# A three-stage fp32 kernel on one core: the low part of the spatial weights by accumulating transfers, stage-two weights stored negated, and a table of 253 offsets

## The chip, the core and the metric

The kernel runs on one core of a Trainium2 chip. Its engines each run their own queue in order: TensorE (PE) multiplies matrices, VectorE (DVE), ScalarE (ACT) and GpSimd (POOL) work on tiles, SyncE (SP) issues most of the DMA transfers and GpSimd a few. The metric is the device time of one execution in microseconds. Before the change three runs gave 916.47, 917.31 and 918.84 us; the median is 917.31.

## The reference

Three blocks follow each other, in float32, for 8 batches of 576 positions:

```
q_s = softmax(q, axis=-1); k_s = softmax(k, axis=seq)      # 8 heads of 64
x   = q_s @ (k_s^T @ v)                                    # block 1: [8, 576, 512]
h   = gelu(x @ w_in); u, v = halves of h                   # block 2: w_in 512 x 1024
v_n = layernorm(v) * g_ln
v_s = einsum('ts,bsd->btd', w_sg, v_n) + b_sg              # w_sg 576 x 576: the spatial weights
x   = x + (u * v_s) @ w_out
h   = relu(x @ w_in2)                                      # block 3
out = (h * sigmoid(conv3(h, conv_w))) @ w_out2
```

The weights of blocks 2 and 3 are read by the kernel as they come, and the first thing done with each is to take it apart into two numbers.

## The kernel before

**Products in three parts.** A float32 product on TensorE is made of three products of a shorter type (fp32r): each operand is a high part, which is the value rounded to that type, and a low part, which is what the rounding left. `mm3` multiplies high by high, high by low and low by high into one accumulator. So every weight and every activation is needed as a pair: `wAh` and `wAl` in the rows are the pair of `w_in`, `wouth` and `woutl` of `w_out`, `sgh` and `sgl` of the spatial weights, `vnh` and `vnl` of the normalized `v`, `gh` and `gl` of the gated product, `xh` and `xl` of a batch's activations.

**Who makes the pairs.** For an activation ScalarE copies the value to the short type (high) and VectorE subtracts (low). For the weights of block 2 (`split`, a job of 1024 columns) ScalarE and VectorE rebuild the value from a 64-bit layout in six steps, ScalarE rounds it, and TensorE then makes the low part of 512 columns in a group of three products into one accumulator: the value times `one` (the unit matrix, a full float32 product), and two products with `neg` (the unit matrix with its sign turned) that subtract the parts that are there; ScalarE copies the result out. One job gives two such groups. The jobs of `w_in` and `w_out` share their working tiles: the tiles `xh` and `xl` of a batch that has not begun, halves of `vnh` and `vnl`, and `wsl`. The rows of the order show `xl` in this part.

**The spatial weights** (`sg_split`, `sg_tail`) come as 4 chunks of 128 x 576 and a tail of 64 x 576, loaded into one `q` tile (the tail into `x2s`). For each chunk ScalarE rounds the high part; for each half of 288 columns TensorE adds raw times `one` and high times `neg` (`part`), and ScalarE copies the result to `sgl`. The tail goes the same way, and its low part is copied to two tiles, `rhs`. That makes ten groups of two products. The bias of the spatial product, `b_sg`, is split by ScalarE and VectorE and sent into two rows of `rhs` by way of DRAM.

**The loops.** Block 1 loads `k`, `v` and `q` per batch, takes maxima and sums on VectorE, subtracts and multiplies on GpSimd, takes exponentials on ScalarE, and `xt` writes `xh` and `xl`. GpSimd's subtraction of the maxima (`kt<-kt,scr`) comes in runs of up to seven instructions that stand in a row. Block 2 runs per batch: `hv` (the products that give `v`, with `norm`), then for each of 8 tiles `hu` (12 products that give `u`), `mx` (14 products with the spatial weights; VectorE multiplies with `u`, ScalarE makes `gh`, VectorE makes `gl`), and `wo` (12 products with `w_out` that read `gh` and `gl`). The sum goes to DRAM as `x2d`, once by a plain transfer and once by a transfer of `xl` that GpSimd issues and that adds to what stands there. While block 2 works on one batch, block 1 of the next is laid between its products. Block 3 reads `x2d` back and repeats per tile: `h2`, the convolution (`cv`), the gate, and `o2`.

**What sets the order.** The kernel's functions do not issue instructions; a recorder (`Plan`) keeps each as a node with what it depends on, and all are issued at the end from one place, so nearly all rows of the profile have one line, L486 (after the change the same place is L488). `price` gives each node a cost, `deadlines` counts back from TensorE's order when each must start, and a table, `MOVED`, adds an offset in microseconds to this due time for chosen nodes (`node:offset`). `order` then plays the program through: whenever an engine is free it takes the ready node that is due first, and TensorE's units of products (a `hu`, an `mx`, a group) are put off while their inputs are late. What an engine has been given by this play it runs in that order on the chip.

## Time and profile before

| what | value |
|---|---|
| median of three runs | 917.31 us (916.47 to 918.84) |
| the profiled execution | 917.11 us, its span 915.3 us |
| TensorE busy | 894.4 us, 98% of the span |
| VectorE, ScalarE, GpSimd busy | 720.7, 536.5, 275.6 us |
| granted TensorE clock in 40 slices of the span | 9 tenths or more in each |

The span is what the profiler saw from the first to the last instruction; the time is counted by the device and lies 1.8 us above it. The busy share is an average over stages: in the first slice of 22.9 us TensorE is busy for five tenths, then for nine tenths or more up to the last slice. Idle time of an engine that nothing waits for costs nothing, which holds for most of what ScalarE and GpSimd have. In the chain that ended last TensorE holds 88% of the span and VectorE 6%, so what remains is to be looked for where TensorE stands still.

### The profile page before, as it was taken

How to read it: one execution, taken by the hardware profiler on the slowest of the kernel's cores; microseconds unless marked ns; L12 is line 12 of the kernel's file. 1: busy time of each engine (PE TensorE's matmuls, PEld its weight loads, DVE VectorE, ACT ScalarE, POOL GpSimd, SP SyncE). 2: the span in 40 equal slices, each digit the busy share in tenths (PEclk: the TensorE clock that was granted, in tenths of full speed). 3: DMA queues.
4: the chain of work that ended last, by engine and by line, in shares of the span. 5: the costliest groups of instructions: out<-in, count | busy, mean ns of one | idle time of the engine just before them, and what ended most of it. 6: DMA issues, size and time to landing. Idle time of an engine off the chain costs nothing.

```text
span 915.3 us, 15835 instructions
## 1 busy us (share of the span) xinstructions
PE 894.4 (98%) x6158; PEld 802.7 (88%) x6158; DVE 720.7 (79%) x1269; ACT 536.5 (59%) x1081; POOL 275.6 (30%) x251
## 2 busy tenths in 40 slices
PE   5999999999999999999999999999999999999997
PEld 4688989988889888898999998988999889888996
DVE  6898998887886898888655389898878878875783
ACT  7886476566456555464524155446677666766673
POOL 5044364644535546374422001102020202020000
PEclk9999999999999999999999999999999999999999
DMA  9932458463743736422857441102021202020001
GB/s 315 273 128 48 136 111 243 114 166 99 185 107 100 201 93 212 107 74 93 226 200 218 129 120 52 47 8 102 6 93 34 76 1 94 6 98 13 13 35 57
DMA packets 51235, 101.50 MB, mean 111 GB/s; under 512 B 8788, under 2 KB 22228, under 8 KB 49368
## 3 DMA queue, kind: packets, MB, share of 16 engines
q1 hardware_dynamic: 46408, 89.87, 30.2%
q0 software_dynamic: 4752, 10.62, 6.9%
q8 instruction: 48, 0.79, 0.4%
q14 instruction: 27, 0.22, 0.1%
HBM read 62.59 MB, written 37.88 MB: 110 GB/s over the span
## 4 chain that ended last, share of the span: by engine, by line
PE 88%; DVE 6%; DMA 3%; ACT 1%; SPq 1%; issue 1%; POOL 0%; POOLq 0%; ACTq 0%; DVEq 0%
PE mm L486 58%; PE acc L486 30%; DVE gl L486 2%; DMA x2d<-xl 1%; DMA wsl<-in_w_in 1%; DMA x2d<-x2s 1%; SPq L486 1%; DMA sgh<-in_q 1%; DVE xl L486 1%; DVE u L486 0%; DVE r L486 0%; DVE scr L486 0%; DVE qm L486 0%; DVE wsl L486 0%; DVE q L486 0%
## 5 line engine op out<-in xcount | busy, mean ns | idle before, releaser
L486 DVE SCALAR_TENSOR_TENSOR cv<-h,cw,cv 128x576 f32<-128x576 f32 x128 | 109.9, 860 | 16.9 <-ACT cv L486 14.5
L486 PE MATMUL acc<-wAh,yl 128*128 128x512 f32 x256 | 101.8, 398 | 0.2 <-DVE yl L486 0.2
L486 PE MATMUL acc<-wAl,yh 128*128 128x512 f32 x256 | 101.0, 395 | 0.0
L486 PE MATMUL acc<-wAh,yh 128*128 128x512 f32 x256 | 100.7, 393 | 0.0
L486 POOL TENSOR_TENSOR q<-q,qm 128x576 f32<-128x576 f32 x56 | 68.8, 1254 | 56.9 <-DVE qm L486 25.5
L486 PE MATMUL mm<-xh,w2h 128*128 128x288 f32 x280 | 83.0, 297 | 0.0
L486 PE MATMUL mm<-xh,w2l 128*128 128x288 f32 x280 | 82.4, 294 | 0.0
L486 PE MATMUL mm<-xl,w2h 128*128 128x288 f32 x280 | 82.4, 294 | 0.0
L486 PE MATMUL acc<-gl,wouth 128*128 128x288 f32 x256 | 76.1, 297 | 3.3 <-DVE gl L486 3.3
L486 PE MATMUL mm<-xh,wAh 128*128 128x288 f32 x256 | 76.5, 299 | 0.0
L486 PE MATMUL acc<-gh,wouth 128*128 128x288 f32 x256 | 76.4, 299 | 0.0
L486 PE MATMUL mm<-sgh,vnh 128*128 128x288 f32 x256 | 76.0, 297 | 0.2 <-DVE u L486 0.2
L486 PE MATMUL acc<-gh,woutl 128*128 128x288 f32 x256 | 75.8, 296 | 0.0
L486 PE MATMUL mm<-xh,wAl 128*128 128x288 f32 x256 | 75.6, 295 | 0.0
L486 PE MATMUL mm<-xl,wAh 128*128 128x288 f32 x256 | 75.6, 295 | 0.0
L486 PE MATMUL mm<-sgh,vnl 128*128 128x288 f32 x256 | 75.5, 295 | 0.0
L486 PE MATMUL mm<-sgl,vnh 128*128 128x288 f32 x256 | 75.4, 295 | 0.0
L486 ACT ACTIVATE gh<-u 128x288 fp32r<-128x288 f32 x64 | 28.1, 442 | 74.0 <-DVE u L486 62.1
L486 ACT ACTIVATE cv<-cv 128x576 f32<-128x576 f32 x64 | 43.7, 683 | 40.7 <-DVE cv L486 40.3
L486 DVE TENSOR_TENSOR gl<-u,gh 128x288 fp32r<-128x288 f32 x64 | 53.1, 834 | 10.7 <-ACT gh L486 10.6
L486 DVE TENSOR_TENSOR u<-mm,u 128x288 f32<-128x288 f32 x64 | 28.9, 453 | 39.6 <-PE mm L486 39.3
L486 POOL TENSOR_TENSOR kt<-kt,scr 128x512 f32<-128x512 f32 (+1 forms) x42 | 47.4, 1150 | 38.0 <-DVE scr L486 25.8
(302 smaller groups left out, 2757.1 us busy)
## 6 DMA issues: line engine op xcount, KB each, us to landing
x2d<-x2s SPq DMA_DIRECT2D x16, 576.0 KB, 4.0
x2d<-xl POOLq DMA_DIRECT2D x8, 1152.0 KB, 9.0
kt<-in_k SPq DMA_DIRECT2D x7, 1152.0 KB, 10.5
q<-in_q SPq DMA_DIRECT2D x28, 288.0 KB, 3.8
xf<-x2d SPq DMA_DIRECT2D x7, 1152.0 KB, 5.2
vt<-in_v SPq DMA_DIRECT2D x7, 1024.0 KB, 8.1
out<-ot SPq DMA_DIRECT2D x28, 256.0 KB, 2.0
wsl<-in_w_in SPq DMA_DIRECT2D x9, 512.0 KB, 5.4
```

The source lines that it names most:

```text
L486: getattr(self.real[n.eng], n.name)(*[val(a) for a in n.args], **{k: val(v) for k, v in n.kw.items()})
```

## The change

**Spatial weights.** The high part is now stored with its sign turned (ScalarE's copy with a factor of -1). `gather` has GpSimd issue a transfer from one tile in SBUF into another that adds to what stands there: high part, negative, onto the raw weights, so that the low part is left in their place. Three such transfers are issued, for chunks 0 and 1, chunks 2 and 3 (576 KB each) and the tail (288 KB). ScalarE copies the result, with a factor of -1, into `sgl` chunk by chunk and into the two `rhs`. The ten groups of TensorE and their twelve copies are gone.

**Sign.** `split` for the weights of block 2 stores all parts negated, with `neg` where `one` stood in the first product of a group; `b_sg` is negated as well. The two Gelu instructions that read these products (`norm` and `hu`) have a factor of -1; where two negated operands meet, the signs cancel.

**Scheduling.** The costs of two kinds of nodes in `price` are changed (a copy with a running sum, a transfer issued by GpSimd), and `MOVED` holds 253 other offsets; the node numbers count anew, since the nodes of the spatial weights differ. A branch `far` in `split` is added that no job uses (`JOBS` holds only `n`).

```diff
-JOBS = 'nnnnnnnnnnnn'
-SGL = 'nnnn'
+JOBS = 'nnnnnnnnnn'
+SGA = ((0, 1), (2, 3))
...
 MOVED = """
-6:-16.1 7:-20.3 9:-42.4 10:-15.1 11:-4.8 12:-5.9 13:5.3 17:-6.7 20:-32.7 28:5.7 31:32.3 35:3.8 41:-15.1 44:4.9 53:-5.4 87:4.4 142:-22.8 166:4.7
...
+6:-45.6 7:-28.9 8:-89.8 9:-47.9 10:-44.5 11:-35.2 13:-33.9 14:-17.7 15:-42.8 20:-50.1 28:-16.7 31:-61.1 32:-44.2 34:-17.8 35:-17.4 37:-24.3 50:-42.6
...
             if "accum_out" in n.kw:
-                n.cost += 0.1
+                n.cost += 0.19
...
             if "dma" in name:
-                n.cost, n.lat = 1.34, 9.3
+                n.kb, n.rate = views[0].ids.size * 4 / 1024, 186
+                n.cost, n.lat = 1.34, 3.1 + n.kb / n.rate
                 return
...
             if n.eng == "pool" and "dma" in n.name:
-                wire[0] = max(t + 1.2, wire[0]) + 6.2
+                wire[0] = max(t + 1.2, wire[0]) + n.kb / n.rate
...
+    def gather(out, part):
+        pool.dma_start(out, r32(part), accum_op=ALU.add, max_dma_last_dim=2304)
+
...
         if hi is not None:
-            act.activation(hi, a, AF.Copy)
+            act.activation(hi, a, AF.Copy, scale=-1.0 if summed else 1.0)
...
         if summed:
-            dve.scalar_tensor_tensor(lo, l, -(2.0 ** -52), hf, ALU.mult, ALU.mult)
+            dve.scalar_tensor_tensor(lo, l, 2.0 ** -52, hf, ALU.mult, ALU.mult)
...
-                pe.matmul(ps, one, cut(a), start=True, stop=False)
+                pe.matmul(ps, r32(neg), cut(a), start=True, stop=False)
                 pe.matmul(ps, neg, cut(hi), start=False, stop=False)
                 pe.matmul(ps, neg, cut(lo), start=False, stop=True)
...
-        act.activation(vt_, ps, AF.Gelu_apprx_tanh)
+        act.activation(vt_, ps, AF.Gelu_apprx_tanh, scale=-1.0)
...
-        act.activation(u, ps, AF.Gelu_apprx_tanh)
+        act.activation(u, ps, AF.Gelu_apprx_tanh, scale=-1.0)
...
     def sg_split(c):
-        hi, lo, raw = sg["hi"][:, c], sg["lo"][:, c], sgr["t"][:, c]
-        act.activation(hi, raw, AF.Copy)
-        if SGL[c] != 'n':
-            E[SGL[c]].tensor_tensor(lo, raw, r32(hi), ALU.subtract)
-        for hf in range(2 if SGL[c] == 'n' else 0):
-            cs = slice(hf * HALF, hf * HALF + HALF)
-            plan.begin()
-            ps = mm_tile()[:, 0:HALF]
-            part(ps, raw[:, cs], hi[:, cs])
-            act.activation(lo[:, cs], ps, AF.Copy)
+        hi, raw = sg["hi"][:, c], sgr["t"][:, c]
+        act.activation(hi, raw, AF.Copy, scale=-1.0)
+        for g in SGA:
+            if c == g[-1]:
+                cs = slice(g[0], c + 1)
+                gather(sgr["t"][:, cs], sg["hi"][:, cs])
+                for i in g:
+                    act.activation(sg["lo"][:, i], sgr["t"][:, i], AF.Copy, scale=-1.0)
 
     def sg_tail():
-        act.activation(rhs1, sgs[:, 0], AF.Copy)
-        for hf in range(2):
-            cs = slice(hf * HALF, hf * HALF + HALF)
-            plan.begin()
-            ps = mm_tile()[:, 0:HALF]
-            part(ps, sgs[:, 0, cs], rhs1[:, cs])
-            for e in range(2):
-                r = slice(64 * e, 64 * e + 64)
-                act.activation(rhs2[e][r, cs], ps[r], AF.Copy)
+        act.activation(rhs1, sgs[:, 0], AF.Copy, scale=-1.0)
+        gather(sgs[:, 0], rhs1)
+        for e in range(2):
+            r = slice(64 * e, 64 * e + 64)
+            act.activation(rhs2[e][r], sgs[r, 0], AF.Copy, scale=-1.0)
...
-
-    def part(ps, x, hi):
-        pe.matmul(ps, one, x, start=True, stop=False)
-        pe.matmul(ps, neg, hi, start=False, stop=True)
```

**TensorE, before, between the last job of `w_in` and the first of `w_out`.** Of a group of three products on `xl` the last one makes the low part; `hu` and `mx` are units of 12 and 14 rows, of which the first two stand here. The names are those of buffers, each with a number.

```order
L486 MATMUL mm_178<-xl_0_184,one_80 128x512
...
L486 MATMUL mm_131<-xl_0_184,one_80 128x512
...
L486 MATMUL mm_152<-xh_0_306,wAh_297 128x288
L486 MATMUL mm_152<-xl_0_327,wAh_297 128x288
...
L486 MATMUL mm_143<-sgh_388,vnh_528 128x288
L486 MATMUL mm_143<-sgl_488,vnh_528 128x288
...
L486 MATMUL mm_178<-xh_0_306,wAh_297 128x288
L486 MATMUL mm_178<-xl_0_327,wAh_297 128x288
...
L486 MATMUL mm_131<-xl_0_184,one_80 128x512
L486 MATMUL mm_131<-wouth_704,neg_96 128x512
L486 MATMUL mm_131<-woutl_711,neg_96 128x512
```

**TensorE, after, the same place.**

```order
L488 MATMUL mm_153<-xl_0_213,neg_96 128x512
...
L488 MATMUL mm_133<-xh_0_313,wAh_301 128x288
L488 MATMUL mm_133<-xl_0_334,wAh_301 128x288
...
L488 MATMUL mm_180<-xl_0_213,neg_96 128x512
...
L488 MATMUL mm_133<-xh_0_313,wAh_301 128x288
L488 MATMUL mm_133<-xl_0_334,wAh_301 128x288
...
L488 MATMUL mm_153<-xh_0_313,wAh_301 128x288
L488 MATMUL mm_153<-xl_0_334,wAh_301 128x288
...
L488 MATMUL mm_180<-xl_0_213,neg_96 128x512
L488 MATMUL mm_180<-wouth_659,neg_96 128x512
L488 MATMUL mm_180<-woutl_662,neg_96 128x512
```

The two groups of the last `w_in` job stood side by side, with a `hu`, an `mx` and a `hu` (38 products) between them and the `w_out` job. Now a `hu` stands between the two groups, and two `hu` (24 products) between the second group and the `w_out` job.

**ScalarE, before, the same place.** `xl<-xh` is the first step of the `w_out` job, `wouth<-xl` its rounding, `wAl<-mm` copies out a low part of the `w_in` job, `u` and `v` read the Gelu products, `lt` belong to the normalized tail.

```order
L486 ACTIVATE wAl_295<-mm_178 128x4x128
L486 ACTIVATE rd_523<-mv_518 128x1
L486 ACTIVATE xl_0_184<-xh_0_166 128x1024
L486 ACTIVATE lt_0_663<-v_465,rd_523 64x512
L486 ACTIVATE lt_0_109<-v_465,rd_523 64x512
L486 ACTIVATE wAl_295<-mm_131 128x4x128
L486 ACTIVATE u_686<-mm_152 128x288
L486 ACTIVATE qx_638<-qm_578 32x72 x3
L486 ACTIVATE wouth_704<-xl_0_184 128x1024
```

**ScalarE, after, the same place.**

```order
L488 ACTIVATE u_620<-mm_133 128x288
L488 ACTIVATE v_464<-mm_161 128x512
L488 ACTIVATE xl_0_213<-xh_0_127 128x1024
L488 ACTIVATE vnh_518<-v_476,rd_615 128x512
...
L488 ACTIVATE lt_0_373<-xl_0_213 128x512
...
L488 ACTIVATE v_476<-acc_0_278 128x512
...
L488 ACTIVATE u_117<-mm_153 128x288
L488 ACTIVATE wsl_192<-wsl_192 128x512
L488 ACTIVATE lt_0_655<-v_464,rd_615 64x512
L488 ACTIVATE lt_0_106<-v_464,rd_615 64x512
L488 ACTIVATE wouth_659<-xl_0_213 128x1024
```

Between the first step of the `w_out` job and its rounding stood five rows, the third of them a copy of a low part; now ten stand there, among them the eviction of a `v` and of a `u` and the steps of another job (`lt<-xl`, `wsl`). The first step stands behind a `u` and a `v` that read TensorE's products.

On VectorE the rows of the same `w_out` job stand like this after the change: `vnl` (reads what ScalarE writes as `vnh` in the fourth row above), two steps on `xl` in one row each, a third one, `lt` (reads what ScalarE writes in the two rows `lt<-v`), a step that writes `xh`, and the last, which writes `woutl`. Before, `lt` stood behind the first step on `xl`, and the other four steps of the job in a row behind it. GpSimd's runs of `kt` subtractions: between the `mx` whose `gl` VectorE makes beside the second of them and the `wo` that reads this `gl`, TensorE had 67 products and now has 27.

## Rows read from the trace of the kernel before

**Rows 1.** The page of the profile: its span, and the first line of its first part.

```profile
span 915.3 us, 15835 instructions
PE 894.4 (98%) x6158; PEld 802.7 (88%) x6158; DVE 720.7 (79%) x1269; ACT 536.5 (59%) x1081; POOL 275.6 (30%) x251
```

**Rows 2.** Timeline of TensorE, 44 to 71 us: start us, duration us, engine, line, instruction.

```profile
44.86 0.65 PE L486 MATMUL mm<-q,one 128*128 128x288 f32 x2
...
45.48 0.65 PE L486 MATMUL mm<-q,one 128*128 128x288 f32 x2
...
60.98 1.02 PE L486 MATMUL mm<-xl,one 128*128 128x512 f32 x2
...
63.63 0.29 PE L486 MATMUL mm<-xh,wAh 128*128 128x288 f32 x1
...
68.66 1.02 PE L486 MATMUL mm<-xl,one 128*128 128x512 f32 x2
...
70.06 0.50 PE L486 MATMUL mm<-woutl,neg 128*128 128x512 f32 x1 [0.15 <-DVE woutl L486]
```

**Rows 3.** By tile (neg, sgl, x2s): count, ns shortest/median/longest, first and last start.

```profile
L486 PE MATMUL mm<-sgh,neg x8: 508/509/513, 45.1 to 56.6; 128*128 128x288 f32 x8
...
L486 ACT ACTIVATE sgl<-mm x8: 410/410/432, 45.7 to 57.2; 128x288 fp32r<-128x288 f32 x8
...
L486 ACT ACTIVATE rhs<-x2s x1: 685/685/685, 36.5 to 36.5; 128x576 fp32r<-128x576 f32 x1
```

**Rows 4.** DMA issues of the page: count, KB each, median us to landing.

```profile
x2d<-x2s SPq DMA_DIRECT2D x16, 576.0 KB, 4.0
x2d<-xl POOLq DMA_DIRECT2D x8, 1152.0 KB, 9.0
```

**Rows 5.** Timeline of ScalarE, 60 to 69 us, columns as in rows 2.

```profile
60.10 0.67 ACT L486 ACTIVATE lt<-xl 128x512 f32<-128x512 f32 x1
...
61.24 0.60 ACT L486 ACTIVATE v<-mm 128x512 f32<-128x512 f32 x1 [0.19 <-PE mm L486]
...
63.36 1.14 ACT L486 ACTIVATE xl<-xh 128x1024 f32<-128x1024 f32 x1 [0.17 <-PE mm L486]
64.41 1.32 ACT L486 ACTIVATE lt<-v,rd 64x512 fp32r<-64x512 f32 x2
...
66.12 0.38 ACT L486 ACTIVATE u<-mm 128x288 f32<-128x288 f32 x1
...
68.03 1.06 ACT L486 ACTIVATE wouth<-xl 128x1024 fp32r<-128x1024 f32 x1 [0.70 <-DVE xl L486]
```

**Rows 6.** Timeline of VectorE, 52 to 70 us, and one row at 28 us.

```profile
28.47 0.69 DVE L486 TENSOR_TENSOR scr<-kt 128x512 f32<-128x512 f32 x1 [0.69 <-DMA kt<-in_k]
...
52.50 0.72 DVE L486 SCALAR_TENSOR_TENSOR vnl<-v,rd,vnh 128x512 fp32r<-128x512 f32 x1
...
64.54 0.69 DVE L486 TENSOR_SCALAR xl<-xl 128x1024 f32<-128x1024 f32 x1 [0.63 <-ACT xl L486]
...
66.77 1.22 DVE L486 SCALAR_TENSOR_TENSOR xl<-xh,xl 128x1024 uint32<-128x1024 uint32 x1
...
68.76 1.24 DVE L486 SCALAR_TENSOR_TENSOR woutl<-xh 128x1024 fp32r<-128x1024 uint32 x1
```

**Rows 7.** Windows: us, busy us (instructions) by engine, granted clock, DMA share, GB/s.

```profile
0.00:45.00 45.00, 32.72 (x217) 23.04 (x218) 33.71 (x66) 34.19 (x75) 13.68 (x28) 1.00 0.93 293
```

**Rows 8.** Timelines of GpSimd and VectorE, 201 to 208 us.

```profile
201.63 6.67 POOL L486 TENSOR_TENSOR kt<-kt,scr 64x256 f32<-64x256 f32 x6 [4.08 <-DVE scr L486]
...
202.78 4.94 DVE L486 TENSOR_TENSOR gl<-u,gh 128x288 fp32r<-128x288 f32 x1
```

**Rows 9.** Timeline of TensorE: its idle times over 0.5 us behind the first 30 us.

```profile
207.77 0.40 PE L486 MATMUL acc<-gl,wouth 128*128 128x288 f32 x1 [1.67 <-DVE gl L486]
...
272.69 0.40 PE L486 MATMUL acc<-gl,wouth 128*128 128x288 f32 x1 [0.58 <-DVE gl L486]
...
338.85 0.40 PE L486 MATMUL acc<-gl,wouth 128*128 128x288 f32 x1 [0.70 <-DVE gl L486]
```

More of the change, by code (lines that the diff above doesn't have):

```diff
@@ L540, in u64, with split @@
         return ap.bitcast(U32)
-    def split(slot, src, hi, lo, n, modes, stores=(), behind=None):
+    def gather(out, part):
+        pool.dma_start(out, r32(part), accum_op=ALU.add, max_dma_last_dim=2304)
+    def split(slot, src, hi, lo, n, modes, stores=(), behind=None, far=False):
         raw, a = slot
@@ L571, in split @@
             return
+        if far:
+            low = slot[0][:, 0:n]
+            if len(src.shape) == 4:
+                low = low.rearrange("p (g f) -> p g f", g=g)
+            gather(a, hi)
+            dve.scalar_tensor_tensor(low, l, 2.0 ** -52, hf, ALU.mult, ALU.mult)
+            gather(a, low)
+            act.activation(lo, a, AF.Copy, scale=-1.0)
+            return
         if summed:
-            dve.scalar_tensor_tensor(lo, l, -(2.0 ** -52), hf, ALU.mult, ALU.mult)
+            dve.scalar_tensor_tensor(lo, l, 2.0 ** -52, hf, ALU.mult, ALU.mult)
             for o in range(0, n, 512):
@@ L1149, in w_job @@
     def w_job(i):
-        split(slots[ORDER[i]], *jobs[i], None if JOBS[i] == 'n' else (E[JOBS[i]], E[JOBS[i]]))
+        split(slots[ORDER[i]], *jobs[i], None, far=JOBS[i] == 'a')
     n1 = len(PAIR[0])
@@ L1187, in sg_tail @@
         sp.dma_start(bt, b_sg.rearrange("(p f) -> p f", f=9))
-        act.activation(bh, bt, AF.Copy)
-        dve.tensor_tensor(bl, bt, r32(bh), ALU.subtract)
+        act.activation(bh, bt, AF.Copy, scale=-1.0)
+        dve.scalar_tensor_tensor(bl, bt, -1.0, r32(bh), ALU.mult, ALU.subtract)
         for i, t in enumerate((bh, bl)):
```

31 rows, old and new, of the table MOVED are left out of this document.

## The prediction

> **What bounds the kernel now.** I read the page first, for its span and for how busy each engine is; then TensorE's own timeline, for the places where it stands still; then the timelines of ScalarE and VectorE around those places. TensorE is busy for 894.4 of 915.3 us [rows 1], so nothing shortens the kernel that does not take work from TensorE or one of its waits. In the windows view the first 45 us hold 32.72 us of TensorE work [rows 7], so some 12 us of its idle time lie there, while inputs and weights arrive at 293 GB/s and are split. Behind that it waits rarely: in the timeline only three idle times are longer than half a microsecond, 1.67, 0.58 and 0.70 us, all for a `gl` of VectorE [rows 9]. The granted clock is 1.00 in the window shown, the upper of its two levels (2.4 GHz), so no term below is about the clock.
>
> **TensorE's own work.** Before, the low part of the spatial weights takes ten groups: eight for the four main chunks (two halves each) and two for the tail [rows 3]. A group is one fp32 product, which the trace shows as two records, and one with `neg`. Two groups in a row start at 44.86 and 45.48 [rows 2], so a group takes 0.62 us, and ten take 6.2 us. No TensorE instruction comes in their place. In the stretch in which they stand TensorE never waits for long, so they lie on the path that sets the end: 6.2 us is the most that this edit can give by itself. The stored sign costs nothing there: the same products run with `neg` in place of `one`, and ScalarE and VectorE undo it by a factor in instructions that they run anyway.
>
> **ScalarE and the transfers.** ScalarE loses eight copies of 0.41 us and four of half the height, and gains six of 576 columns, 0.69 us each by the one in the trace [rows 3]: 12 times 0.41 against 6 times 0.69 is 0.8 us less, off the path. GpSimd issues three accumulating transfers, of 576, 288 and 576 KB. The trace has no accumulation within SBUF. Its nearest rows are 4.0 us for 576 KB without an addition and 9.0 us for 1152 KB with one [rows 4]; I take 6 us for 576 KB, near the middle. All three are issued in a row on GpSimd, and behind them stands the first power of the normalization; as they leave before that power's input exists, nothing queues. Their results are read on ScalarE by four copies that stand behind a table load and two evictions, and TensorE reads them some 10 us later still. So I count them as hidden. If each took the 9.0 us and ran behind the other, ScalarE would stand up to 3 us, and every weight eviction queued behind it as well: that is the upper end of this term, and zero the lower.
>
> The Trainium skill ("SBUF — State Buffer", section "Who interferes with whom" and the box on the trap above it) speaks against this: descriptors of a transfer issued from GpSimd are written by GpSimd's cores, which a VectorE instruction in a two-port mode locks out, so such a transfer can look several times longer beside a busy VectorE. Here VectorE is busy 33.71 of the first 45 us [rows 7]. The accumulations into `x2d` run beside a VectorE that is busy as well and still land in 9.0 us at the median [rows 4], so this trace does not show the trap; by the rule the sum would be up to 3 us longer, the upper end just given.
>
> **What is late next.** The rows of the program's order in the section on the change matter more than the removed work. M is the last weight job of the first matrix, two groups that read the tile `xl`; the first job of the output weights writes the same tile. Before, that job's first ScalarE step waits for TensorE's last read, starts at 63.36 [rows 5], and its last result arrives for TensorE at 70.06 [rows 2]. Between the two jobs TensorE has work from 63.63 to 68.66, 5.0 us, and so it is 0.3 us late: the first group ends at 70.06 plus 0.23, 1.63 us behind its start, where the two groups of M take 2.65 us together.
>
> After the change only two `hu` units stand between them (24 matmuls of 288 columns; the 38 matmuls from 63.63 to 68.66 give 0.13 each, so 1.6 us for the 12 of a unit), and the job's first ScalarE step stands behind the evictions of the first of these two and of the `v` product. So I count from the end of that first `hu`. ScalarE: `u` 0.38, `v` 0.60, the absolute value 1.14 [rows 5], end at 2.1. VectorE has a `vnl` ahead that waits for one more ScalarE step of some 0.7, and takes 0.72 itself: 3.5. Then two steps of 0.69 and one of 1.22 [rows 6]: 6.1. Its next row, `lt`, needs the first of ScalarE's two `lt`; ten ScalarE instructions stand ahead of `wouth`, by rows 5 0.67, 0.60, 0.38, 0.67 and 1.32 and some small ones, so `lt` comes at about 5.7 and `wouth` ends at 7.4. VectorE goes on with `lt` (as `vnl`, 0.72) to 6.8, one step of 0.7 to 7.5, and `woutl` 1.24 to 8.8. TensorE had the second `hu` until 1.6 and the group of 1.3 until 2.9; it can end the group only at 8.8 plus 0.2. It waits 6.1 us where it waited 0.3: I take +5.7. Bounds: 4.4 if `lt` and `vnl` cost VectorE no waiting, and 8 if GpSimd's subtractions, which now run in that stretch, stretch two VectorE steps by a microsecond each.
>
> **The head.** VectorE takes the key maxima (three rows as that at 28.47, 0.69 us each [rows 6], and a pair of half height) behind the weight splits and no longer between them, so the last of the four first jobs can be ready 2 to 3 us earlier. Against it, a 512 KB weight block is now loaded ahead of the value tiles, 1.8 us at 293 GB/s [rows 7]. Bounds: 2.8 us earlier, 1.8 later. Between its first attention product and the first `hv` TensorE has the same work in both orders, and an earlier weight only helps where it waits for one; so I take little, -0.6, a fifth of the gain's bound.
>
> **The rest** is ordered anew all through by the new offsets, with the same instructions. I take 0 with a bound of 3 us on either side, the sum of the three waits in rows 9.
>
> **Sum.** The profiled execution took 917.1 us, its span of 915.3 and 1.8 around it, and lies 0.2 below the median of the runs (917.31). 917.1 - 6.2 + 5.7 - 0.6 = 916.0.
>
> **Rivals.**
> - The saving stands. If the wait at the output-weight pair is no longer than before, 917.1 - 6.2 - 0.6 gives 910.3; if half of it is hidden, because the head brings the output weights in early enough and ScalarE runs ahead, 913.2. For it: 6.2 us of work really goes. Against it: the order of ScalarE's queue is fixed, and the chain above starts from a TensorE result.
> - GpSimd holds VectorE oftener. GpSimd's run of six subtractions from 201.63 lasts 6.67 us, and a `gl` of VectorE with 288 columns takes 4.94 beside it [rows 8], where a VectorE row with 512 takes 0.72 [rows 6]; that is the wait of 1.67. What decides is how much work TensorE has between `mx` and the `wo` that reads this `gl`. For the second of six such runs the order had 8.9 us of it (67 matmuls at 0.13) and now has 3.6 (27), for the last 12 and now 5.2. From 6.7 us on a run is hidden; at 3.6 it costs 3.1. If the five later runs cost 3.1 and four times 1.67, they cost 9.8 where rows 9 sum to 2.95: 916.0 + 6.8 = 922.8, slower. It is slower by the bound below from 6.9 us on in all.
>   The Trainium skill ("SBUF — State Buffer", "SBUF: two separate sides") says that the loser of the shared port blocks for one whole instruction of the other; the row shows that the `gl` lost to a whole run of them. By the rule a `gl` would lose a sixth of the run, 1.1 us, a time and this rival would vanish; by the row it stands.
> - The transfers land late and ScalarE stands, 3 us as bounded: 919.0. Against it: TensorE needs the result only 10 us later.
>
> **How the numbers follow.** About 0.3% (2.75 us) is what a measurement of this kernel can tell from no change: 914.6 to 920.1. Forecast, most of the saving given back at one new wait: 0.46, with a range of its own of 914 to 918.5. The saving stands wholly or by half: 0.36. GpSimd's runs: 0.12. Late transfers: 0.06. Faster takes the second case and 0.06 of the forecast, its lower edge: 0.42. Slower takes the runs, 0.12. The same is the other 0.40 of the forecast with the late transfers, 0.46. The range reaches to the deeper half of the second case below, 911.0, and to 920.0 above; some 0.1 is left out on each side.
>
> **What would show it.** TensorE's rows lose the ten groups with `q` or `x2s` and `one`, and its busy time falls by about 6. The first group with `wouth` and `neg` has an idle time of some 6 us in front of it or within it, with VectorE or ScalarE named. The four copies into `sgl` show no wait for a transfer over 1 us. The three accumulations land within 4 to 9 us. A `gl` of 4 to 5 us beside each run of subtractions shows whether the third rival grew. The forecast is wrong if the two jobs are further apart in time than their places say, if the first `hv` ends more than 2 us earlier than 44.9, or if the sum of waits for `gl` behind 150 us changes by more than 3.

## The result and the profile after

The changed kernel takes 923.62 us in the median of six runs, the one before 917.35 beside it. The ratio is 1.0064, with a 95% interval of 1.0052 to 1.0076: 0.64% slower. The forecast was 916.0, in a range of 911 to 920, so it was wrong in its sign and in its range.

The first lines of the page of the kernel after; rows 1 has those of before.

```profile
span 921.3 us, 15787 instructions
PE 894.0 (97%) x6128; PEld 799.8 (87%) x6128; DVE 730.3 (79%) x1269; ACT 538.6 (58%) x1077; POOL 280.3 (30%) x254
```

The ten groups are gone, and with them some 6 us of products, yet TensorE is busy for 894.0 us where it was 894.4 [rows 1]. Part of its work therefore ran slower. The windows of the kernel after show where (us, busy us and instructions of TensorE, its weight loads, VectorE, ScalarE, GpSimd, then the granted clock, the DMA share and GB/s):

```profile
62.00:64.00 2.00, 0.00 (x0) 0.00 (x0) 1.93 (x5) 1.95 (x5) 0.00 (x0) 1.00 0.00 0
66.00:68.00 2.00, 1.62 (x2) 0.30 (x2) 1.78 (x4) 2.00 (x3) 0.00 (x0) 0.67 0.00 0
68.00:70.00 2.00, 1.58 (x4) 0.93 (x4) 1.97 (x3) 1.97 (x3) 0.00 (x0) 0.50 0.00 0
...
74.00:76.00 2.00, 2.00 (x18) 2.00 (x17) 1.65 (x3) 1.95 (x5) 0.00 (x0) 1.00 0.00 0
...
406.00:408.00 2.00, 1.25 (x10) 1.01 (x9) 2.00 (x5) 0.00 (x0) 0.05 (x1) 1.00 0.00 0
408.00:410.00 2.00, 2.00 (x10) 2.00 (x10) 1.97 (x6) 1.41 (x2) 0.00 (x0) 0.51 0.62 220
```

At 62 us TensorE does nothing at all for two microseconds, and behind that its clock stands at 0.50, the lower of its two levels (1.2 GHz). It does so again at 408 us. The same two places in TensorE's timeline; the rows at 66.38 and 69.27 answer to 68.66 and 70.06 in rows 2, and the last two to no wait of before [rows 9]:

```profile
61.65 0.29 PE L488 MATMUL mm<-xh,wAl 128*128 128x288 f32 x1
66.38 1.80 PE L488 MATMUL mm<-xl,neg 128*128 128x512 f32 x2 [4.43 <-DVE xl L488]
69.27 0.80 PE L488 MATMUL mm<-woutl,neg 128*128 128x512 f32 x1 [0.41 <-DVE woutl L488]
...
72.42 0.45 PE L488 MATMUL mm<-xh,wAh 128*128 128x288 f32 x1
72.66 0.45 PE L488 MATMUL mm<-xl,wAh 128*128 128x288 f32 x1
...
405.52 0.40 PE L488 MATMUL acc<-gl,wouth 128*128 128x288 f32 x1 [1.99 <-DVE gl L488]
407.20 0.40 PE L488 MATMUL acc<-gh,wouth 128*128 128x288 f32 x1 [0.75 <-DVE x2s L488]
```

The first output-weight group waits 4.43 us for `xl` and 0.41 for `woutl`, and behind it two products start 0.24 us apart instead of 0.13. To see what this is worth, the span is cut at four products that both orders have: the first of block 1's `hu` (`xh` with `wAh`), and the 9th, the 161st and the 201st of `acc<-gh,wouth` (a `wo` has four, so these begin the third, the 41st and the 51st `wo`). Starts read from TensorE's timelines, us:

| stretch | before | after | difference |
|---|---|---|---|
| start to the first `hu` | 48.65 | 47.45 | -1.2 |
| first `hu` to third `wo` | 40.34 | 44.57 | +4.2 |
| third to 41st `wo` | 292.57 | 292.56 | 0.0 |
| 41st to 51st `wo` | 70.15 | 73.39 | +3.2 |
| 51st `wo` to the end | 463.6 | 463.3 | -0.3 |

Four of the ten groups stood ahead of the first `hu` (2.5 us by the forecast's 0.62) and six behind it (3.7). In the second stretch the wait grew from 0.15 to 4.84, and some 6.4 us of work at half clock cost 3.2: 40.34 - 3.7 + 4.7 + 3.2 = 44.5, as measured. (Four `scr` products, 0.4 us, stand ahead of the first `hu` in the new order and behind it in the old; three late starts at 47.5 to 48.2 us make up for them in this sum.) That is an account by TensorE's rows and not yet a cause; the experiments ask which of its terms decides. In the text below, E1 is the second stretch, first `hu` to third `wo`, and E2 is the fourth.

### The profile page after: what moved, and what is told of

Read it like the earlier page. It is cut to its first block, busy times and chain, and to the rows that moved or that the text cites. A ratio compares the mean times of both kernels' runs of the same rounds, so it can differ in the third digit from the quotient of the medians.

```text
span 921.3 us, 15787 instructions
## 1 busy us (share of the span) xinstructions
PE 894.0 (97%) x6128; PEld 799.8 (87%) x6128; DVE 730.3 (79%) x1269; ACT 538.6 (58%) x1077; POOL 280.3 (30%) x254
## 4 chain that ended last, share of the span: by engine, by line
PE 90%; DVE 3%; ACT 3%; issue 1%; DMA 1%; POOL 0%; SPq 0%; POOLq 0%; DVEq 0%; ACTq 0%
PE mm L488 59%; PE acc L488 31%; ACT L488 1%; DMA q<-in_v 1%; DMA sgl<-in_k 1%; DVE wsl L488 0%; ACT q L488 0%; DVE xl L488 0%; DVE gl L488 0%; ACT v L488 0%; DVE qm L488 0%; ACT kt L488 0%; ACT xh L488 0%; DVE scr L488 0%; ACT xl L488 0%
## 5 line engine op out<-in xcount | busy, mean ns | idle before, releaser
L488 DVE SCALAR_TENSOR_TENSOR cv<-h,cw,cv 128x576 f32<-128x576 f32 x128 | 114.1, 894 | 16.7 <-ACT cv L488 14.5
L488 POOL TENSOR_TENSOR kt<-kt,scr 128x512 f32<-128x512 f32 (+1 forms) x42 | 49.8, 1208 | 33.7 <-issue 27.2
L488 DVE TENSOR_TENSOR cv<-cv,h 128x576 f32<-128x576 f32 x64 | 48.2, 755 | 14.3 <-ACT cv L488 13.4
```

What stands on the lines that cost most here:

```text
L488: getattr(self.real[n.eng], n.name)(*[val(a) for a in n.args], **{k: val(v) for k, v in n.kw.items()})
```

## The experiments

Each kernel below has the instructions of the kernel after, in an order that is written out, so that one thing moves at a time; two add products that nobody reads, and two leave out the transfers. The diffs show the rows of one engine's queue. Ratios are to the kernel before, with 95% intervals.

**Place two: the `gl` behind GpSimd's run.** VectorE's rows in the kernel after, and GpSimd's beside them:

```profile
397.11 0.71 DVE L488 STREAM_TRANSPOSE scr<-r 128x512 f32<-128x512 f32 x1
...
399.57 5.89 DVE L488 TENSOR_TENSOR gl<-u,gh 128x288 fp32r<-128x288 f32 x1
```

```profile
398.12 5.91 POOL L488 TENSOR_TENSOR kt<-kt,scr 64x256 f32<-64x256 f32 x5
```

The transposition releases GpSimd's run of five, and a `gl` some rows behind it on VectorE, 0.45 us long elsewhere, ends at 405.46, 1.4 us past the run's end. In rows 8 it was like that: the `gl` there took 4.94 us and ended within 0.6 us of the run's end. `gl_first` puts the transposition behind the `gl`.

```diff
 VectorE
-STREAM_TRANSPOSE scr<-r 128x512
 TENSOR_SCALAR wsl<-wsl 128x512
 TENSOR_TENSOR u<-mm,u 128x288
 ...
 TENSOR_TENSOR gl<-u,gh 128x288
+STREAM_TRANSPOSE scr<-r 128x512
```

> The kernel after, with one VectorE row moved: the transposition that lets GpSimd's subtractions at 398 us begin stands behind the gl that now takes 5.89 us beside them. Theory A: this gl takes 0.5 us, the 2.75 us in which TensorE waits at 403 to 407 us go, and with them the 3.4 us at half clock (1.7 us): 919.2 (918.3 to 920.2). Theory B (GpSimd's run only moves, and the next gl is held instead): 922 to 924.

Measured: 920.38 us, 1.0031 (1.0018 to 1.0044). The same `gl` and the row that now stands beside the run:

```profile
398.74 0.45 DVE L500 TENSOR_TENSOR gl<-u,gh 128x288 fp32r<-128x288 f32 x1
399.11 0.70 DVE L500 STREAM_TRANSPOSE scr<-r 128x512 f32<-128x512 f32 x1
...
402.98 4.12 DVE L500 TENSOR_SCALAR wsl<-wsl 128x512 uint32<-128x512 uint32 x1
```

E2 falls from 73.39 to 70.33 us, against 70.15 before, and the low clock behind it is gone. The hold itself stays, 4.12 us on a `wsl`; of it TensorE sees only a wait of 0.69 for the next `gl`. Not every VectorE row is held: beside the same run `qm`, `x2s` and `u` took their usual 0.74, 0.81 and 0.46 us. So half of the loss is this one row. The other half is untouched: the third `wo` begins at 92.00 us, and at 92.02 in the kernel after.

**Place one: is it the low clock?** `warm_pair` has TensorE run 30 products that nobody reads while it waits, `warm_more` 50.

```diff
 TensorE, ahead of the first output-weight group
+MATMUL mm<-xh,wAh 128x288 x30
 MATMUL mm<-xl,neg 128x512
```

> The kernel after, with 30 more products of 288 columns (4.0 us at 0.13 each) ahead of the first output-weight group: they write the accumulator that the group then clears, so no result depends on them, and they fill most of the 4.4 us in which TensorE waits there. Theory A (what the clock lost came from that wait): the group starts where it did, at about 66.4 us, the granted clock stays 1.00 behind it, and the 6.8 us at half clock vanish, which is 3.2 to 3.4 us less: 920.3 (919.6 to 921.0). Theory B (the low clock has another cause, or the wait alone costs): 923.6, as the kernel after.

Measured: 924.22 us, 1.0077 (1.0052 to 1.0101). No gain in the time: the clock held until 71.2 us, but TensorE waited 1.60 for `wouth` and 0.71 for `woutl`, and the clock fell for 3.41 us behind those.

> As warm_pair, with 50 filling products in place of 30 (6.6 us), so that the first output-weight group begins when all its inputs are there and TensorE never stands still before it. Theory A2 (the low clock costs only what TensorE has to do after the chain has ended: 69.3 to 73.2 us at half clock): the clock stays 1.00 and the time is 2 us less than that of the kernel after, 921.6 (920.8 to 922.5). If the clock costs nothing there: 923.6.

Measured: 924.34 us, 1.0058 (1.0037 to 1.0078). TensorE's row with `woutl` of the first output-weight group, and the window behind it:

```profile
71.50 0.50 PE L503 MATMUL mm<-woutl,neg 128*128 128x512 f32 x1 [0.68 <-DVE woutl L503]
```

```profile
72.00:73.00 1.00, 1.00 (x4) 0.48 (x4) 0.93 (x4) 0.96 (x3) 0.00 (x0) 1.00 0.00 0
```

The clock is at 1.00, and the product takes 0.50 us, as in rows 2, where it took 0.80 at half clock. The time did not fall, but that does not acquit the clock, for in both kernels another row changed too. GpSimd's power `rd`, and the ScalarE row that waits for it and stands ahead of `wouth`, here in `gl_first` (which has the same rows up to there and no filling products) and in `warm_more`:

```profile
66.26 0.55 POOL L500 TENSOR_TENSOR rd<-rd,nhalf 128x1 f32<-128x1 f32 x1 [3.49 <-ACT rd L500]
66.94 1.32 ACT L500 ACTIVATE lt<-v,rd 64x512 fp32r<-64x512 f32 x2
```

```profile
66.27 1.64 POOL L503 TENSOR_TENSOR rd<-rd,nhalf 128x1 f32<-128x1 f32 x1 [3.50 <-ACT rd L503]
67.94 1.34 ACT L503 ACTIVATE lt<-v,rd 64x512 fp32r<-64x512 f32 x2 [0.87 <-POOL rd L503]
```

The power took 1.64 us instead of 0.55 (in `warm_pair` as well; why is not shown), so `wouth` and `woutl` came 1.0 us later. What the clock is worth shows behind the product with `woutl`, where all inputs of the group are there. The order from there to the third `wo` is the same in these kernels, and the low clock behind the wait for `xl`, 6.83 us long in all but the first, began at other moments: in `gl_first` while TensorE still waited,

```profile
65.00:67.00 2.00, 0.00 (x0) 0.00 (x0) 1.93 (x3) 1.97 (x7) 0.55 (x1) 0.56 0.00 0
72.00:74.00 2.00, 2.00 (x13) 1.67 (x12) 1.48 (x4) 0.88 (x3) 0.79 (x1) 0.99 0.00 0
```

and in the kernel after only behind the wait. Read from the timelines and from windows of half a microsecond, us (`old_head` comes below):

| kernel | product with `woutl` | half clock behind it | from it to the third `wo` |
|---|---|---|---|
| `warm_more` | 71.50 | 0 | 20.79 |
| `gl_first` | 70.47 | 1.6 | 21.53 |
| `old_head` | 77.97 | 2.5 | 21.98 |
| after | 69.27 | 4.2 | 22.75 |

Each microsecond at half clock costs close to half a microsecond, and in the kernel after the low clock at the pair costs 2.0 us of the account's 3.2. The other 1.2 were hidden: they passed while the chain to `woutl` was still under way. In `warm_more` the 2.0 were gained, and the later `rd` took 1.0 of them, so that E1 is 43.65; its first `hu` began 1.2 us later than in the kernel after, and the third `wo` at 92.29.

The second place shows the same. These kernels have the same order there and the same two waits of TensorE, 1.99 and 0.71 to 0.75 us:

| kernel | half clock behind the waits | E2 |
|---|---|---|
| `chain_first` (below) | 0 | 71.85 |
| after | 3.41 | 73.39 |
| `warm_more` | 6.83 | 74.49 |

`chain_first`, behind its second wait:

```profile
410.57 0.40 PE L503 MATMUL acc<-gh,wouth 128*128 128x288 f32 x1 [0.75 <-DVE x2s L503]
```

```profile
410.00:412.00 2.00, 1.43 (x10) 1.43 (x11) 2.00 (x6) 0.06 (x1) 0.00 (x0) 1.00 0.00 0
```

So of E2's 3.2 us the waits are 1.7 and the clock 1.5. These are single profiles. No kernel here removed the clock's cost at the pair and showed the gain in its time: `warm_more` lost it again, 1.0 at `rd` and 1.1 in E2.

**Is it one row, or the job's place, in the queues?** `vnh_first` moves one `vnh` ahead of two rows on ScalarE. `early_job` moves the first steps of the output-weight job on ScalarE and VectorE ahead of the normalization rows.

```diff
 ScalarE, vnh_first
+ACTIVATE vnh<-v,rd 128x512
 ACTIVATE wAl<-mm 128x4x128
 ACTIVATE u<-mm 128x288
-ACTIVATE vnh<-v,rd 128x512
```

> The kernel after, with one ScalarE row moved: the vnh at 57.8 us stands ahead of a copy of a low part and of a u, both of which wait for TensorE there. Theory A (the chain that ends at the first output-weight group runs through ScalarE's order): vnh starts at about 56.1, what follows on VectorE is 1.7 us earlier, and so is the group: 921.9 (921 to 923), and the low clock stays. If the chain does not run through this row: 923.6.

Measured: 923.62 us, 1.0075 (1.0056 to 1.0093); the wait stays at 4.43. This `vnh`, at 57.8 us, ran ahead of the chain: the `u` with which the chain begins waits for TensorE at 60.40.

```diff
 VectorE, early_job
+TENSOR_SCALAR xl<-xl 128x1024 x2
+SCALAR_TENSOR_TENSOR xl<-xh,xl 128x1024
+TENSOR_SCALAR xh<-xl 128x1024
+SCALAR_TENSOR_TENSOR woutl<-xh 128x1024
 BN_STATS st<-v 128x6
 ...
-TENSOR_SCALAR xl<-xl 128x1024 x2
 ...
```

> The kernel after, with six steps of the first output-weight job further ahead in the queues of ScalarE (two) and VectorE (four rows); nothing else moves. Theory A: the wait at the first output-weight group goes from 4.9 us to under 2, and the clock behind it stays 1.00, so both 3 to 4 us of wait and 3.3 us of clock are gone: 917 (915.5 to 918.5). Theory B (only the length of the wait counts): 920. If the steps that are pushed back make a later wait of the same size, 923.6.

Measured: 927.38 us, 1.011 (1.0085 to 1.0135). TensorE's waits in it:

```profile
65.78 2.04 PE L500 MATMUL mm<-xl,neg 128*128 128x512 f32 x2 [2.21 <-DVE xl L500]
...
75.58 0.61 PE L500 MATMUL mm<-xh,wAh 128*128 128x288 f32 x1 [5.22 <-ACT woutl L500]
```

The wait at the pair is halved, and a longer one comes behind it; E1 is 47.5. What is brought forward pushes something else back.

**Is it the transfers?** `after_no_sums` is the kernel after without the three accumulating transfers, `old_no_sums` the same in the old order.

> The kernel after without its three accumulating transfers (the low part of the spatial weights is left out of what is computed). Theory C (in the kernel after the wait at 62 to 69 us is the chain through ScalarE and VectorE, and no row waits more than 0.7 us for these transfers): 923 (922 to 924), with the wait of 4 to 5 us still there. Theory D (the transfers delay loads here too, as they do in the old order, where leaving them out gave 6.3 us): 917 to 920.

Measured: 923.75 us, 1.006 (1.0042 to 1.0078), with the wait of 4.43 still there. In the new order no cost of the transfers is seen in the time, though its profile has 6.83 us of low clock at the second place (E2 74.43), which could cover a microsecond.

**The same instructions in the old order.** `old_order` and `old_order2` emit the kernel after in the order of the kernel before; the second has the last copies into `sgl`, and those into `rhs`, later on ScalarE:

```diff
 ScalarE
 ACTIVATE rd<-mv 128x1
-ACTIVATE sgl<-q 128x576 x2
 ...
 ACTIVATE v<-acc 128x512
+ACTIVATE sgl<-q 128x576 x2
```

> All instructions of the kernel after in the order of the kernel before: the ten groups and their copies are left out, the three accumulating transfers follow their high parts, ScalarE's copies stand where evictions of the groups stood, two loads of q wait for them. Theory A (the edit saves what TensorE's groups took, and the new order lost it again): 917.4 - 6.2 = 911.2 (910 to 912.5). Theory B (the accumulating transfers or what waits for them give the saving back, whatever the order): 915 to 918.

Measured: 922.38 us, 1.0056 (1.0034 to 1.0079), with a wait of 5.54 on ScalarE for the first transfer, so the place that I had given the copies seemed to decide it.

> As old_order (the instructions of the kernel after in the order of the kernel before), but with ScalarE's copies of the first two chunks, which stood 5.54 us for their transfer there, some eight rows later, and the two loads of q that need them behind these. Theory A (old_order lost its saving to that stall, which comes from where the copies stand, and the saving itself is real): the wait of 7.0 us and the low clock behind it go, 922.4 - 7.0 - 3.4 = 912 (911 to 913.5). Theory C (up to 75 us ScalarE and VectorE set the pace, and what is taken from TensorE there comes back as its waiting): 915 to 918, with waits of 4 us or more of TensorE before 75 us for VectorE or ScalarE.

Measured: 923.15 us, 1.0065 (1.0053 to 1.0077). Moving the copies only moved the wait. ScalarE's timeline and TensorE's:

```profile
49.01 0.71 ACT L503 ACTIVATE vnh<-v,rd 128x512 fp32r<-128x512 f32 x1
56.83 0.23 ACT L503 ACTIVATE xh<-xh 128x24 f32<-128x24 uint32 x1 [7.12 <-DMA xh<-in_conv_w]
```

```profile
58.32 2.08 PE L503 MATMUL mm<-one,r 128*128 128x128 f32 x8 [7.58 <-DVE r L503]
```

A load of 24 KB, the convolution's weights, lands late, and ScalarE's next row is its conversion; everything behind stands 7 us. `old_no_sums` asks whether that is the transfers' doing:

> old_order2 without the three accumulating transfers: ScalarE's copies then take the raw weights, so the low part of the spatial weights is left out of what is computed. Theory A: the transfers are hidden where the copies stand late enough, so 912 as old_order2, within 1. Theory D (they cost by what they take from the loads beside them): 1 to 3 us less than old_order2.

Measured: 916.83 us, 0.999 (0.9974 to 1.0005): 6.3 us less than `old_order2`, so in that order the three transfers cost 6.3 us. The small load is issued at 45.58 us in it and lands in 4.5; in `old_order2` it is issued at 49.23 and lands in 7.6. The run also shows what the removal of the ten groups gives by itself: 0.1%, not clear of nothing, and not 0.7%. TensorE waits in it instead:

```profile
38.02 1.13 PE L503 MATMUL mm<-xl,neg 128*128 128x512 f32 x2 [1.02 <-DVE xLl L503]
...
48.06 0.40 PE L503 MATMUL mm<-xh,wAl 128*128 128x288 f32 x1 [1.25 <-ACT wAl L503]
...
51.90 1.16 PE L503 MATMUL mm<-one,r 128*128 128x128 f32 x8 [0.50 <-DVE r L503]
...
62.23 0.40 PE L503 MATMUL mm<-xh,wAl 128*128 128x288 f32 x1 [1.90 <-ACT wAl L503]
```

These four sum to 4.67 us, and each names VectorE or ScalarE. `conv_late` keeps the transfers and moves the three small rows that read the load behind the first `wo`:

```diff
 ScalarE
 ACTIVATE vnh<-v,rd 128x512
-ACTIVATE xh<-xh 128x24
 ACTIVATE u<-mm 128x288
-ACTIVATE xh<-xh 128x24
 ...
 ACTIVATE kt<-kt 128x768
+ACTIVATE xh<-xh 128x24 x2
 VectorE
-TENSOR_SCALAR xh<-xh 128x24
 ...
+TENSOR_SCALAR xh<-xh 128x24
```

> old_order2 with three small rows of ScalarE and VectorE moved behind the first wo: those that need the load of the convolution's weights, for which ScalarE stood 7.12 us there. Theory D1 (the price of the transfers in the old order is this one late load, for which everything queued behind on ScalarE waited): 916.8 as old_no_sums (915.5 to 918). Theory D2 (the transfers take their time from all loads): another load is waited for, 920 to 923.

Measured: 915.82 us, 0.9975 (0.9962 to 0.9987), 7.3 less than `old_order2` (some 8 by the ratios), so the price of the transfers was this load. The change in the old order, with these rows moved, is thus 0.25% faster than before, and the new order costs it some 8 us. E1 is 41.5 us: still 1.2 longer than before, though six groups of it are gone. One wait in it is longer than a microsecond, and the clock falls for 3.41 us behind it, some 1.7 us of work more:

```profile
61.27 0.40 PE L503 MATMUL mm<-xh,wAl 128*128 128x288 f32 x1 [1.98 <-ACT wAl L503]
```

```profile
62.00:64.00 2.00, 2.00 (x11) 2.00 (x10) 1.77 (x4) 2.00 (x3) 0.74 (x1) 0.52 0.00 0
```

Why the saving came back as waits is seen where the ten groups had stood. The windows from 45 to 62 us, in the kernel before, in `conv_late` and in the kernel after:

```profile
45.00:62.00 17.00, 17.00 (x90) 13.80 (x89) 15.76 (x25) 14.38 (x35) 9.88 (x10) 1.00 0.57 188
```

```profile
45.00:62.00 17.00, 14.04 (x71) 10.48 (x70) 16.56 (x26) 13.67 (x30) 10.67 (x11) 1.00 0.87 280
```

```profile
45.00:62.00 17.00, 16.95 (x92) 13.45 (x91) 12.84 (x19) 11.36 (x24) 9.45 (x9) 1.00 0.99 302
```

Before, TensorE was full and VectorE busy for 15.76 of 17 us. In the old order without the groups VectorE is full, 16.56 us, and TensorE stands for 3.0. In the kernel after it is the other way round: TensorE is full up to 62 us and VectorE is not, and what the new order loses comes behind, at the pair.

**Can the rows be placed better?** `paced` moves off-path rows on ScalarE and VectorE (the `qm` maxima, `wsl`, `lt`) behind the output-weight job, in the old order. `chain_first` does the like in the new one: the normalization rows first, and two `mx` ahead of the output-weight pair on TensorE.

> conv_late with ScalarE's, VectorE's and GpSimd's rows between 52 and 70 us in another order: three maxima of q (2.06 us of VectorE), their copies, and two first steps of later weight jobs behind the first output-weight job; the powers of the normalization ahead of one of GpSimd's subtractions each; the low part of the last w_in job and the last v ahead of rows that aren't needed yet. TensorE's order is not touched. Theory C (between 38 and 75 us ScalarE and VectorE set the pace, so that TensorE's 6.2 us came back as waits): with some 3 us taken out of their chain the time falls by 2 to 4 us below conv_late, 914 (912.5 to 915.5) if that is 916.8. If TensorE's own work sets the pace: no change from conv_late.

Measured: 918.67 us, 1.0008 (0.9994 to 1.0022), a miss: the first `wo` comes 2 us earlier in its profile, but 1.5 of that stood ahead of the first `hu` already, and the third is not earlier (E1 43.3, against 41.5). What was put off on VectorE is then due, as I read it; no run shows that.

> The kernel after with another order between 54 and 72 us: on ScalarE, VectorE and GpSimd the rows of the normalization (rd, vnh, v, vnl, lt) of the last three tiles as early as their inputs allow, ahead of the first output-weight job; on TensorE two mx ahead of that job's two groups. Theory E (the new order holds the normalization by one late rd row, and so leaves TensorE without an mx to run there): the first mx starts at 63 to 65 us, where it started at 74.5, the waits of 62 to 69 us together fall to under 3 us, and the time by 4 to 6 us: 918.5 (917 to 920). Theory C (ScalarE and VectorE lack the time, in whatever order): a wait of the same size elsewhere before 80 us, 922 to 924.

Measured: 925.31 us, 1.0071 (1.0053 to 1.0089). The wait at the pair has gone, and three others have come:

```profile
67.07 0.40 PE L503 MATMUL mm<-sgh,vnh 128*128 128x288 f32 x1 [1.75 <-ACT vnh L503]
...
70.83 0.61 PE L503 MATMUL mm<-sgh,vnh 128*128 128x288 f32 x1 [2.29 <-DVE u L503]
...
82.65 0.40 PE L503 MATMUL mm<-xh,wAh 128*128 128x288 f32 x1 [1.26 <-ACT woutl L503]
```

Its window from 50 to 75 us, and before's beside it:

```profile
50.00:75.00 25.00, 20.69 (x109) 17.30 (x108) 23.81 (x34) 19.04 (x38) 11.12 (x11) 0.90 0.55 178
```

```profile
50.00:75.00 25.00, 24.85 (x141) 20.49 (x140) 22.78 (x37) 20.97 (x45) 11.40 (x12) 1.00 0.19 62
```

VectorE is busy for 23.81 of 25 us, and was for 22.78 before. With the wait at the pair taken away, VectorE is as full here as in the old order.

**All such waits together.** `old2_gl`, `chain_gl` and `conv_gl` are `old_order2`, `chain_first` and `conv_late` with transpositions moved behind the `gl` as in `gl_first` (three in the old order, for the three waits in rows 9; one in the new).

> old_order2 with three VectorE rows moved: each transposition that starts a run of GpSimd's subtractions stands behind the gl that was held 4.6 to 4.9 us beside it (203, 268, 334 us in the kernel before). Theory A: the waits of 1.67, 0.58 and 0.70 us go, and no gl is held in their place for long: 2 to 3 us below old_order2, 909 to 910 if that is 912. If the runs only hold the next gl: as old_order2.

> chain_first with the one row of gl_first (the transposition at 397 us behind the gl). Theory E with A: both gains add, 3 to 4 us below chain_first: 915 (913.5 to 916.5). Theory C with A: 919 to 920.5, as gl_first.

> conv_late (the old order) with three transpositions behind the gl that GpSimd's subtractions hold. If waits of 1.67, 0.58 and 0.70 us go and only smaller ones come, as between old_order2 and old2_gl: 1 to 2 us below conv_late, 914.3 (913 to 915.5). If the time there is set elsewhere: 915.8.

Measured: 921.58 us, 1.0045 (1.0032 to 1.0059); 921.62, 1.0039 (1.0024 to 1.0054); and 914.41, 0.9966 (0.9952 to 0.9979). They are 1.6, 3.7 and 1.4 us below the kernels that they stem from. The last is 0.8 by the ratios, whose intervals overlap, so it is not clear of nothing; of the 3.7, 1.5 stand in E2, where `chain_first` has no low clock. `conv_gl` is the best here, and beats both kernels; the same move was not tried on the kernel before. Of the waits for `gl` in rows 9 (2.95 us), these are left in it, beside one of 0.34 for `gh`:

```profile
282.02 0.40 PE L503 MATMUL acc<-gl,wouth 128*128 128x288 f32 x1 [0.49 <-DVE gl L503]
...
347.84 0.40 PE L503 MATMUL acc<-gl,wouth 128*128 128x288 f32 x1 [0.92 <-DVE gl L503]
```

**Head or stretch?** Three kernels exchange the first part of the order. `old_head` has all ahead of the first product of `q` and `kvd` in the old order and the rest in the new, `old_to_hu` all ahead of the first `hu`, `new_head` the converse of `old_head`.

```diff
-order: new throughout, with gl_first's move
+old_head:  conv_late's first 183 instructions, then the others in the new order
+old_to_hu: conv_late's first 371 instructions, then the others in the new order
-order: old throughout, as conv_gl
+new_head:  the first 183 of the new order, then the others in conv_gl's
```

> The kernel after, with the transposition of the second wait moved (as in gl_first), and in it everything that stood ahead of the first product of q and kvd in the old order (conv_late's) emitted in that order; behind it the new order. It asks whether the late start of that product in the new order (23.0 to 25.2 us in the profiles, 20.1 to 21.6 in the old order) sets the end. Theory H, the head is on the path: the product starts at 20 to 21.6 and the time falls by 1.4 to 2.4 from gl_first's 920.4, to 918 to 919. Theory M, what the head brings in earlier is waited away between 45 and 75 us, where VectorE sets the pace: the product starts earlier, the third wo still at about 92.0, time 920.4. Theory N, the pieces fit badly and a new wait comes at the seam: over 921.

> As old_head, but all that stood ahead of the first product of block 1's hu (xh with wAh, 46.1 us in conv_late, 47.5 in the kernel after) is emitted in the old order, the rest in the new one with the moved transposition. From that product to the third wo the profiles give 43.4 us in gl_first, 44.6 in the kernel after, and 41.5 in conv_late, so the new order loses 1.9 to 3.1 us behind the product and 1.4 (up to 4.7 against conv_gl) ahead of it. Theory H, the loss stands ahead: third wo at 87.5 to 90, time 916 to 918.5. Theory M, the loss stands behind, whatever comes earlier: third wo at about 92, 920 to 921, with a wait of 4 us or more at the output-weight group as in the kernel after.

> The converse: conv_gl's order, but all that stands ahead of the first product of q and kvd in the new order is emitted in the new order, and then the rest in the old one. Theory H: the product starts at 23 to 25 and the time rises by 1.4 to 2.4 from conv_gl's 914.4, to 916 to 917. Theory M: the product is late and the rest makes up for it, 914.4 and no more than 0.7 beside it.

Measured: 928.84 us, 1.0112 (1.0091 to 1.0132); 921.83, 1.0045 (1.0028 to 1.0061); 923.29, 1.0052 (1.0034 to 1.0071). All three have new waits at the seam; in `old_head` ScalarE stands 5.48 us for a small load, and TensorE 8.55:

```profile
28.87 0.21 ACT L503 ACTIVATE bh<-bt 64x9 fp32r<-64x9 f32 x1 [5.48 <-DMA bt<-in_b_sg]
```

So what the head is worth can't be read from their times. E1 can be read, for it starts behind the seam (in `old_to_hu` at it). From the timelines, us:

| order ahead of the first `hu`, behind it | kernel | first `hu` | E1 |
|---|---|---|---|
| new, new | after | 47.45 | 44.57 |
| new, new | `gl_first` | 48.64 | 43.36 |
| new, new | `after_no_sums` | 50.32 | 43.40 |
| old up to `q` and `kvd`, new | `old_head` | 56.14 | 43.81 |
| old, new | `old_to_hu` | 48.83 | 46.41 |
| old, old | `conv_late` | 46.09 | 41.51 |
| old, old | `conv_gl` | 43.97 | 41.61 |
| old, old | `old_no_sums` | 46.39 | 41.88 |
| new up to `q` and `kvd`, old | `new_head` | 56.33 | 40.98 |

With the new order behind the first `hu` E1 takes 43.4 to 46.4 us (a wait of 1.53 at the seam is in the last), whatever came ahead and however late, and the wait at the pair is 4.43 or 4.44; with the old order it takes 41.0 to 41.9. In `old_to_hu`:

```profile
69.56 1.74 PE L503 MATMUL mm<-xl,neg 128*128 128x512 f32 x2 [4.44 <-DVE xl L503]
```

The loss in E1 thus belongs to the new order of this stretch itself, 1.5 to 5 us of it. Of that, 0.7 to 2.0 us are the low clock behind its wait.

## Why the prediction was wrong

**The step that failed worst is "so no term below is about the clock".** The reason given was that the clock stood at 1.00 in a window of the kernel before, but the same forecast put a wait of 6.1 us into the kernel after, more than three times the longest that the rows behind 30 us show (1.67, rows 9). The clock fell behind both new waits, and that cost 2.0 us at the pair and 1.5 at 408 us, by the two tables above: 3.5 of the 7.1 us by which the profiled span missed the forecast (+6.0 where -1.1 was forecast).

**"The rest ... I take 0"** is the second. It held the wait for one `gl` beside GpSimd's run, worth 1.7 us without its clock. As a rival, GpSimd holding VectorE was given a chance of 0.12 and a price of 6.8 for five runs of six. One run of the six did it, and with its clock it makes half of the loss, shown by `gl_first`. The other waits for `gl` over half a microsecond shrank (0.58 where rows 9 has 2.95), yet the stretch in which they lie kept its 292.6 us. By the rule of the Trainium skill that the forecast weighed ("SBUF — State Buffer", "SBUF: two separate sides") a `gl` would lose one instruction of the run, by estimate a fifth of 5.91 us, so 1.2; this trace does not agree, the `gl` of 0.45 us took 5.89.

**The first term, "so they lie on the path",** was right in part. Ahead of the first `hu` the four groups' 2.5 us are there in the old order: `hu` begins at 48.65 in the kernel before and at 44.0 to 47.1, in the middle at 46.1, in seven kernels with the old order and no groups (one of them without the transfers). Behind it none of the six groups' 3.7 us came back as time in the old order, since VectorE was full: E1 was 40.34 before and is 41.0 to 41.9. That TensorE does not wait is no sign that its work sets the time: two engines can be full side by side. The 894.4 of 915.3 us on the page [rows 1] is a mean over stages, and I applied it to the one stage in which VectorE is nearly as full, 15.76 of 17 us. That window was in the trace before, and the forecast did not read it. So `old_no_sums`, which has neither transfers nor the new order, gains 0.7 of the 6.2 us, and `conv_late` 2.2.

**The new wait** came as forecast, and not by luck: the rows of the chain fell as they were counted. The product with `woutl` begins 9.07 us behind the end of the first `hu` (60.20 to 69.27), where the forecast had 8.8 plus 0.2. TensorE waited 4.84 in all instead of 6.1, because its own group ran at half clock and took 2.5 us instead of 1.3.

**The transfers** were counted as hidden. In the new order no run speaks against it (`after_no_sums`), with 8.8 us at the median where I took 6:

```profile
q<-sgh POOLq DMA_DIRECT2D x2, 576.0 KB, 8.8
...
x2s<-rhs POOLq DMA_DIRECT2D x1, 288.0 KB, 7.9
```

It hung on the order: 6.3 us in `old_order2`, through a load that the forecast did not name.

**The head** was to gain 0.6 beside the 2.5 us of the four groups ahead of the first `hu`; together they gave 1.2 us in the profile (0.4 more without the `scr` products that moved there). `conv_late` and `conv_gl`, equal up to there, are 2.1 us apart in their profiles, so one profile does not tell a term of this size. Eight kernels with the new order up to there, the kernel after among them, begin the first `hu` at 47.5 to 49.6 us, in the middle at 48.4, and the seven with the old one at 44.0 to 47.1. So the new order loses some 2 us here as well, about what the four groups gave.

What stays open: whether rows of the new order can be moved so that the wait at the pair goes and no other comes. Moving one `vnh`, the output-weight job, or the normalization did not do it, and neither did leaving out the transfers. Nor do the runs tell which rows cost the 2 us ahead of the first `hu`, or why `rd` was slow beside the filling products.

## What to carry to other kernels

Price a new wait of TensorE with what the clock does behind it: here that doubled the cost of one wait and was 2.0 us at the other. Read it from places that have the same order and the same wait but another clock, and when a filler gains nothing, look for a row that changed beside it. Price removed work by the engine that paces the stage in which it stands, not by the engine that is busiest over the whole run: where another is within a tenth of full in a window of that stage, expect the saving to come back as waits. When transfers are added, look for small loads behind them and for the row of an in-order engine that reads each; putting those rows off gave 7.3 us here. And a row that releases a run on GpSimd belongs behind the short VectorE row that TensorE needs next.

## What the runs showed of the hardware

TensorE's granted clock fell to 0.50 for 6.83 us with an idle time of 4.43 us, 0.3 us behind its end in the kernel after and 2.4 us ahead of its end in `gl_first`. With idle times of 1.99 and 0.71 to 0.75 us close together it fell for 3.41 us in the kernel after, for 6.83 in `warm_more`, and not at all in `chain_first`; it did not fall behind the 1.67 us of rows 9. In `old_order2`, after 7.58 us, it stayed low for 10.24. Work on the path lost close to half of the time at the low clock.

A VectorE product of two tensors, 0.45 us alone, took 5.89 beside five GpSimd subtractions in a row; a `TENSOR_SCALAR` of 0.42 took 4.12 beside such a run, while a `TENSOR_REDUCE` and products that read TensorE's results kept their usual times there. An accumulating transfer of 576 KB within SBUF landed in 8.8 to 10.5 us at the median, where a plain one to DRAM takes 4.0 [rows 4].
